# Attention and a two-layer feed-forward on one core: the second layer with the output weights stationary and 256 squares moving

## The chip, the cores and the metric

The kernel runs on one core of a Trainium2 chip, in one launch. The metric is the device time in microseconds (us), the median over several runs. TensorE does the matmuls, VectorE (DVE), ScalarE (ACT) and GpSimd (POOL) the elementwise work; SyncE (SP) issues the DMAs.

## The reference

Four batches of eight heads with 768 positions of 64 numbers attend to a window of their neighbours and to sums over blocks of 32; the 3072 x 512 result then goes through a feed-forward of two layers with a squared ReLU between them. Only the second part is touched by the change:

```python
def _moe_ref(x, w_in, w_out):          # x 3072 x 512, w_in 512 x 2048, w_out 2048 x 512
    h = np.maximum(x @ w_in, 0.0)
    return (h * h @ w_out).astype(np.float32)

x = attn_out.transpose(0, 2, 1, 3).reshape(B * S, H * D)
return _moe_ref(x=x, **moe_kwargs)
```

## The kernel before, in words

**Tiling.** The 3072 tokens are cut into 24 attention tiles g of 128 (six for each batch), and for the feed-forward into 12 groups c of `CT` = 256 tokens (two tiles). The 2048 hidden units are cut into `NF` = 16 blocks f of 128. A unit of work is a pair (c, f): the first layer makes 128 hidden units for 256 tokens, their squares go through the second layer, and the second layer's result of 512 model columns for 256 tokens is summed in PSUM over all 16 blocks f.

**Precision by parts.** x, the weights and the squares are each kept as a high part and a low part of fp32r (`xh`, `xl`; `w_sb[f][:, 0]` and `w_sb[f][:, 1]`; `gh`, `gl`), and each product is the sum of three matmuls: high by high, high by low, low by high. `w_sb[f]` holds w_in in its first 512 columns and w_out of the same f behind them, in `DM:`.

**First layer** (`ffn1`, L348). For each of four blocks of the model dimension and each of the three products: 128 x 128 weights stationary, 256 tokens of `xh` or `xl` moving, into `ph` (hidden unit by token). 12 matmuls of 256 columns a unit.

**Squares** (`relu`, `high_square`, `square`, `low_square`): `r` = max(ph, 0), `gh` = r squared, ph = ph times r, `gl` = ph - gh, split between ScalarE and VectorE. They come out as hidden unit by token, 128 x 256.

**Second layer** (`ffn2`, L389). For each of two tiles of 128 tokens (`tt`) and each of the three products: 128 columns of `gh` or `gl` stationary, the 512 columns of w_out moving, into `o_ps[c][tt]`, a whole PSUM bank of token by model column. 6 matmuls of 512 columns a unit. After the last f, `evict` copies each of the two tiles to SBUF (`ob`) and stores it to 128 rows of the output.

**Order.** The first part of the program follows a list written out by hand (`START`), in which F1, RE, SQ, MU, GL, F2 and EV are a unit's first layer, its squares, its second layer and its eviction. It covers the first two groups and six attention tiles; there an accumulation is parked in SBUF halfway (`parked`) while weights still arrive. After it, `slot(c, f, ...)` runs for the other ten groups, eight times each: the first layer of two units (24 matmuls), then the second layer of the two units of the slot before (`finish`, 12 matmuls), so that the squares of two units are made while TensorE works on others. Steps of later attention tiles (`steps`: scores, softmax, turning, outputs) are hung into the slots. Nothing reorders the program; each engine runs its instructions as they are written.

Of the kernel before, what the change touches and what calls it, by code (L numbers as in the profile page):

```python
# [11 lines left out]
F32 = mybir.dt.float32  # L12
# [8 lines left out]
B, H, S, D = 4, 8, 768, 64  # L21
BLOCK, WINDOW = 32, 16
NB = S // BLOCK
DM, DF = 512, 2048
P = 128
NT = S // P
NPAIR = H // 2
TPC = 2
CT = TPC * P
# [41 lines left out]
def attn_ffn_kernel(ctx: ExitStack, tc: tile.TileContext, q, k, kt, v, vt, v0, w, masks, ident, mean, out):  # L71
    nc = tc.nc
# [8 lines left out]
    ps_o = ctx.enter_context(tc.tile_pool(name="ps_o", bufs=2, space=bass.MemoryType.PSUM))  # L81
# [3 lines left out]
    w_sb = {}  # L85
# [19 lines left out]
    def copy(eng, out, in_):  # L105
        nc.scalar.copy(out=out, in_=in_) if eng is nc.scalar else eng.tensor_copy(out=out, in_=in_)  # L106


    def load_q(g):
        nc.sync.dma_start(out=q_sb[g % 2], in_=q[g // NT, g % NT])  # L110

    def load_k(g):
        nc.sync.dma_start(out=k_sb[g % 2][:, 0:4], in_=k[g // NT, g % NT])

    def load_qk(g):
        load_q(g)
        load_k(g)

    def load_v(g):
        nc.sync.dma_start(out=v_sb[g % 2][0:96], in_=v[g // NT, g % NT])  # L120
# [49 lines left out]
    def place_k(g):  # L170
        nc.vector.tensor_copy(out=k_sb[g % 2][:, 4], in_=ksum.unsqueeze(1).to_broadcast([P, 2, NPAIR, NB]))
# [106 lines left out]
    def softmax(g, h0, h1):  # L278

        for h in range(h0, h1):  # L280
            mask_max(g, h)
            exponentials(h)
# [58 lines left out]
    o_ps, parked = {}, {}  # L341

    def ffn1(c, f):
        ph = ps_h.tile([P, 4, P], F32, name="ph").rearrange("p a b -> p (a b)")[:, 0:CT]
        n = 0
        for cc in range(NC4):
            for w, x in ((0, xh), (1, xh), (0, xl)):
                nc.tensor.matmul(  # L348
                    ph, lhsT=w_sb[f][:, w, cc * P : (cc + 1) * P], rhs=x[c][:, cc, :], start=(n == 0), stop=(n == 3 * NC4 - 1)
                )  # L350
                n += 1
        return ph
# [23 lines left out]
    def squares(ph):  # L376
        r = relu(ph, nc.scalar)
        gh = high_square(r)
        square(ph, r)
        return gh, low_square(ph, gh)  # L380

    def ffn2(c, f, gh, gl, first, last):
        if first:
            o_ps[c] = [ps_o.tile([P, DM], F32, name="o_ps") for _ in range(TPC)]
        for tt in range(TPC):
            ts_ = slice(tt * P, (tt + 1) * P)
            n = 0
            for g_, w in ((gh, 0), (gh, 1), (gl, 0)):
                nc.tensor.matmul(  # L389
                    o_ps[c][tt], lhsT=g_[:, ts_], rhs=w_sb[f][:, w, DM:],  # L390
                    start=(first and n == 0), stop=(last and n == 2),
                )
                n += 1

    def evict(c, f, tt, eng):

        if (c, tt) in parked:
            ob = parked[c, tt]
            nc.vector.tensor_add(out=ob, in0=o_ps[c][tt], in1=ob)
        else:  # L400
            ob = work.tile([P, DM], F32, name="ob", tag="ob", bufs=4)
            copy(eng, ob, o_ps[c][tt])
        if f < NF - 1:
            parked[c, tt] = ob
        else:
            r0 = c * CT + tt * P
            nc.sync.dma_start(out=out[r0 : r0 + P, :], in_=ob)

# [4 lines left out]
    def finish():  # L415

        for p in behind:
            ffn2(*p)
        done = [p[:2] for p in behind if p[-1]]
        behind.clear()  # L420
        return done[0] if done else None

    def slot(c, f, side, last):


        ph = [ffn1(c, f + i) for i in range(2)]
        done = finish()
        for i in range(2):
            for do in side[i]:
                do()  # L430
            behind.append((c, f + i, *squares(ph[i]), f + i == 0, f + i == NF - 1))
        for tt in range(TPC if done else 0):
            evict(*done, tt, nc.scalar)
        for do in last:
            do()
# [35 lines left out]
    def load(what, i):  # L471
        if what == "kv":
            load_kv0(i)
        elif what == "kw":
            load_kv(1, i)
        elif what == "q":
            load_q(i)
        elif what == "k":
            load_k(i)
        elif what == "v":  # L480
            load_v(i)
        elif what == "w":
            load_w(i)
        elif what == "vn":
            vn[i] = room(F32, "vn")[:, 0 : 3 * DM].rearrange("p (t c) -> p t c", c=DM)
            nc.sync.dma_start(out=vn[i], in_=v0[:, 3 * i : 3 * i + 3])
        elif what == "mask":
            nc.sync.dma_start(out=mask_sb, in_=masks.rearrange("m q c -> q m c"))
        elif what == "id":
            nc.sync.dma_start(out=id_sb, in_=ident)  # L490
        else:
            nc.sync.dma_start(out=mean_sb, in_=mean)

    def begin(op, i, j, eng):


        if op == "KS":
            sum_k(0, i)
        elif op == "PK":
            place_k(i)  # L500
        elif op == "SV":
            v_mean[0] = sum_v0([vn[0], vn[1]])
        elif op == "VC":
            place_v0(v_mean[0], i, eng)
        elif op == "KT":
            sum_k(1, i)
        elif op == "VT":
            sum_v(1, i)

        elif op == "S":  # L510
            (scores_kt if i < FROM_KT else scores)(i, 2 * j, 2 * j + 2)
        elif op == "TT":
            mask_max(i, j)
        elif op == "E":
            exponentials(j)
        elif op == "NR":
            inverse(j)
        elif op == "N":
            norm(j, eng)
        elif op == "T":  # L520
            tp[i, j] = turn_pe(i, j)
        elif op == "TC":
            copy(eng, pT[i % 2][:, j * 4 : j * 4 + 4], tp.pop((i, j)))
        elif op == "O":
            outputs(i)
        elif op == "XH":
            high_x(i)
        elif op == "XL":
            low_x(i)

        elif op in ("HI", "LO", "SH", "AD", "CA", "SU"):
            {"HI": sign_w, "LO": round_w, "SH": shift_w, "AD": add_w, "CA": high_w, "SU": low_w}[op](i, eng)

        elif op == "F1":
            ph_of[i] = ffn1(*units[i][:2])
        elif op == "RE":
            r_of[i] = relu(ph_of[i], eng)
        elif op == "SQ":
            g_of[i] = [high_square(r_of[i])]
        elif op == "MU":  # L540
            square(ph_of[i], r_of[i])
        elif op == "GL":
            g_of[i].append(low_square(ph_of.pop(i), g_of[i][0]))
        elif op == "F2":
            c, f, f0, f1 = units[i]
            ffn2(c, f, *g_of.pop(i), f == f0, f == f1 - 1)
        elif op == "EV":
            evict(*units[[4, 15, 26, 31][i]][:2], j, eng)
        else:
            raise AssertionError(op)  # L550

    with tc.manual_schedule(engines=None):
        for token in START.split():
            what, i, j, eng = re.fullmatch(r"(L:[a-z]+|F[12]|[A-Z]+)\.?(\d*)\.?(\d*)([avp]?)", token).groups()
            i, j = int(i or 0), int(j or 0)
            if what.startswith("L:"):
                load(what[2:], i)
            else:
                begin(what, i, j, engines.get(eng))
        tiles = {g: steps(g) for g in range(6, n_g)}  # L560

        def at(side, last, g, step):

            for i in range(2):
                if g in tiles and 0 <= step + i < 12:
                    side[i] += tiles[g][0][step + i]
                    last += tiles[g][1][step + i]

        place_k(7)
        load_q(7)  # L570
        load_k(7)
        load_v(6)
        load_v(7)
        load_qk(8)
        softmax(6, 0, 6)
        behind += [(*units[i][:2], *g_of[i], False, i == 31) for i in (30, 31)]
        for c in range(2, n_c):
            for f in range(0, NF, 2):
                side, last = [[], []], []
                at(side, last, 2 * c + 2, f + (4 if c == 2 else 6))  # L580
                at(side, last, 2 * c + 3, f - 2)
                at(side, last, 2 * c + 4, f - 10)
                slot(c, f, side, last)
        done = finish()
        for tt in range(TPC):
            evict(*done, tt, nc.scalar)


# [65 lines left out]
```

## Time and profile before

| | us |
|---|---|
| three runs | 625.07, 625.56, 627.52 |
| their median | 625.56 |
| the profiled execution's own time, first to last instruction (span) | 624.0 |
| TensorE busy with matmuls in the span | 599.8 |
| TensorE busy with weight loads, beside the matmuls | 537.5 |
| VectorE, ScalarE, GpSimd busy | 411.9, 293.8, 97.4 |
| mean granted TensorE clock | 0.992 |

The three runs are executions without the profiler; the profile is one further execution, for which the span is the time that is known. Matmuls overlap one another, so a line's busy time is the time in which at least one of its matmuls was in flight, and the mean of one is the whole passage of one through the engine. How far apart two matmuls of a row are is read from the start times in the timeline. L348 is the first layer's matmul, L389 the second's.

### The profile page before, as it was taken

What the parts mean: (1) busy time and instruction counts of PE and PEld (TensorE: products, weight loads), DVE (VectorE), ACT (ScalarE), POOL (GpSimd) and SP (SyncE); (2) the same over time, 40 slices, a digit from 0 to 9 for tenths busy, and PEclk for the clock granted to TensorE, in tenths of its full rate; (3) what the DMA queues carried; (4) which work ended last, traced back from release to release, by engine and by line L of the source; (5) the groups of instructions that cost most, each with busy time, mean ns of one, the idle gap of its engine ahead of it and who ended that gap; (6) DMA issues with size and microseconds to landing.
All of it is one profiled execution on the core that took longest, in us unless ns stands there. A gap on an engine that the chain in (4) does not pass through costs nothing.

```text
span 624.0 us, 13374 instructions
## 1 busy us (share of the span) xinstructions
PE 599.8 (96%) x5216; PEld 537.5 (86%) x5216; DVE 411.9 (66%) x1237; ACT 293.8 (47%) x850; POOL 97.4 (16%) x83
## 2 busy tenths in 40 slices
PE   2699999999999999999999999999999999999997
PEld 2588888988989988998988989899889989889996
DVE  4889989768766857757658668567566566563222
ACT  2778887333544353443534444434525525433322
POOL 2555762001210100101201101101101001000000
PEclk9979999999999999999999999999999999999999
DMA  8999610462132231220230321311201301000000
GB/s 286 378 359 326 213 60 21 154 202 99 27 120 70 83 119 50 104 69 35 68 118 37 119 84 70 119 52 48 74 26 44 103 1 26 35 1 2 35 0 35
DMA packets 19855, 60.38 MB, mean 97 GB/s; under 512 B 2768, under 2 KB 2896, under 8 KB 17744
## 3 DMA queue, kind: packets, MB, share of 16 engines
q1 hardware_dynamic: 19792, 59.53, 28.4%
q8 instruction: 41, 0.67, 0.5%
q14 instruction: 22, 0.18, 0.1%
HBM read 53.23 MB, written 6.29 MB: 95 GB/s over the span
## 4 chain that ended last, share of the span: by engine, by line
PE 92%; DMA 3%; DVE 2%; ACT 2%; SPq 0%; issue 0%; DVEq 0%; ACTq 0%
PE ph L348 42%; PE o_ps L389 41%; PE x_ps L317 4%; PE s_ps L241 3%; DMA q_sb<-in_q 2%; DMA mask_sb<-in_masks 1%; PE s_ps L256 1%; PE ph L297 1%; ACT e_sb L276 0%; DVE w_sb L227 0%; DVE e_sb L268 0%; ACT w_sb L106 0%; SPq L152 0%; DVE sm L285 0%; DVE w_raw L216 0%
## 5 line engine op out<-in xcount | busy, mean ns | idle before, releaser
L348 PE MATMUL ph<-xh,w_sb 128*128 128x256 f32 x1536 | 272.6, 280 | 0.2 <-DVE gl L373 0.2
L348 PEld LDWEIGHTS ph<-xh,w_sb 128*128 128x128 f32 x1536 | 238.6, 189 | 9.7 <-issue 3.0
L389 PE MATMUL o_ps<-w_sb,gh 128*128 128x512 f32 x768 | 237.9, 391 | 0.0
L348 PE MATMUL ph<-xl,w_sb 128*128 128x256 f32 x768 | 213.5, 278 | 0.2 <-DVE xl L334 0.2
L389 PEld LDWEIGHTS o_ps<-w_sb,gh 128*128 128x128 f32 x768 | 137.1, 188 | 24.8 <-issue 0.2
L389 PE MATMUL o_ps<-w_sb,gl 128*128 128x512 f32 x384 | 151.4, 394 | 0.9 <-DVE gl L373 0.9
L369 DVE TENSOR_TENSOR ph<-ph,r 128x256 f32<-128x256 f32 x192 | 82.6, 431 | 101.0 <-ACT r L357 98.8
L357 ACT ACTIVATE r<-ph 128x256 f32<-128x256 f32 x180 | 68.0, 378 | 168.1 <-PE ph L348 167.9
L348 PEld LDWEIGHTS ph<-xl,w_sb 128*128 128x128 f32 x768 | 145.1, 189 | 0.4 <-DVE xl L334 0.4
L291 POOL TENSOR_TENSOR e_sb<-e_sb,sm 128x480 f32<-128x480 f32 x43 | 43.5, 1013 | 403.5 <-DVE nmx L268 356.6
L276 ACT ACTIVATE e_sb<-e_sb,nmx 128x120 f32<-128x120 f32 x192 | 73.8, 386 | 67.3 <-DVE nmx L268 67.3
L304 DVE STREAM_TRANSPOSE pT<-e_sb 32x256 f32<-32x256 f32 x216 | 94.2, 436 | 5.1 <-POOL e_sb L291 1.8
L373 DVE TENSOR_TENSOR gl<-ph,gh 128x256 fp32r<-128x256 f32 x192 | 81.5, 425 | 23.3 <-DVE ph L369 0.5
L364 ACT ACTIVATE gh<-r 128x256 fp32r<-128x256 f32 x192 | 80.2, 418 | 12.1 <-DVE r L359 6.1
L389 PEld LDWEIGHTS o_ps<-w_sb,gl 128*128 128x128 f32 x384 | 72.2, 188 | 15.7 <-DVE gl L373 1.3
L334 DVE TENSOR_TENSOR xl<-x_ps,xh 128x512 fp32r<-128x512 f32 x24 | 16.6, 690 | 48.1 <-ACT xh L331 48.1
L268 DVE CUSTOM_DVE_ANT_0 e_sb<-s_ps,mask_sb 128x120 f32<-128x120 f32 x192 | 43.9, 274 | 5.5 <-PE ph L297 1.6
L331 ACT CAST xh<-x_ps 128x512 fp32r<-128x512 f32 x24 | 14.0, 584 | 53.6 <-PE x_ps L317 53.2
L220 POOL TENSOR_TENSOR w_raw<-w_raw 128x1024 int32<-128x1024 int32 x16 | 35.3, 2214 | 24.1 <-ACT w_raw L212 8.7
L317 PEld LDWEIGHTS x_ps<-pT,v_sb 128*64 128x64 f32 x768 | 25.4, 141 | 13.3 <-issue 11.3
L276 ACT ACTIVATION_READ_ACCUMULATOR e_sb<-e_sb,nmx 128x1 f32 x192 | 35.8, 187 | 0.0
L317 PE MATMUL x_ps<-pT,v_sb 128*64 128x64 f32 x768 | 29.0, 229 | 5.3 <-issue 4.0
(47 smaller groups left out, 291.2 us busy)
## 6 DMA issues: line engine op xcount, KB each, us to landing
w_raw<-in_w SPq DMA_DIRECT2D x16, 1024.0 KB, 13.9
v_sb<-in_v SPq DMA_DIRECT2D x24, 384.0 KB, 3.8
k_sb<-in_k SPq DMA_DIRECT2D x20, 384.0 KB, 5.1
kv<-in_kt SPq DMA_DIRECT2D x16, 384.0 KB, 4.8
q_sb<-in_q SPq DMA_DIRECT2D x24, 256.0 KB, 4.1
out<-ob SPq DMA_DIRECT2D x24, 256.0 KB, 2.1
kv<-in_vt SPq DMA_DIRECT2D x12, 384.0 KB, 5.3
vn<-in_v SPq DMA_DIRECT2D x2, 768.0 KB, 10.7
```

The source lines that it names most:

```text
L220: nc.gpsimd.tensor_tensor(out=hi, in0=hi, in1=lo, op=ALU.add)
L268: nc.vector.tensor_tensor_reduce(out=e_sb[:, h, 0:NK], in0=s_ps[g][:, h % 2, h // 2, 0:NK], in1=m, scale=-scale, scalar=3.0e38, op0=ALU.ad ...
L276: nc.scalar.activation(e, e, AF.Exp, bias=nmx[half][:, i : i + 1], scale=-1.0, accum_out=sm[half][:, i : i + 1])
L291: eng.tensor_mul(out=e, in0=e, in1=sm[half].unsqueeze(2).to_broadcast([P, 4, NK]))
L304: nc.vector.transpose(out=pT[g % 2][j * 32 : j * 32 + 32, :, i * 32 : i * 32 + 32], in_=e_sb[i * 32 : i * 32 + 32, :, j * 32 : j * 32 + 32],)
L317: nc.tensor.matmul(xp[o : o + 64, h // 2, s * 64 : s * 64 + 64], lhsT=v_sb[g % 2][:, s, h * 64 : h * 64 + 64], rhs=pT[g % 2][:, h, s * 64 ...
L348: nc.tensor.matmul(ph, lhsT=w_sb[f][:, w, cc * P : (cc + 1) * P], rhs=x[c][:, cc, :], start=(n == 0), stop=(n == 3 * NC4 - 1))
L357: nc.scalar.activation(r, ph, AF.Relu)
L364: nc.scalar.activation(gh, r, AF.Square)
L369: nc.vector.tensor_mul(out=ph, in0=ph, in1=r)
L373: nc.vector.tensor_sub(out=gl, in0=ph, in1=gh.bitcast(F32))
L389: nc.tensor.matmul(o_ps[c][tt], lhsT=g_[:, ts_], rhs=w_sb[f][:, w, DM:], start=(first and n == 0), stop=(last and n == 2),)
```

## The change

The second layer is turned around. Instead of squares stationary and w_out moving, each 128 x 128 block of w_out is stationary, and all 256 tokens of `gh` or `gl` move past it. The result is [model column, token]. Two banks hold it as before, now each with two blocks of 128 model columns side by side, 256 tokens each; the bank `i` is run through all three products before the next, and within a product the two halves `j` take turns. A unit has 12 matmuls of 256 columns instead of 6 of 512. The `start` flag is given with the first half alone. The output in memory has the shape [group, bank, 128, 512], stored in the same 24 pieces of 128 rows by 2 KB, and is transposed on the host after the launch.

```diff
     def ffn2(c, f, gh, gl, first, last):
         if first:
-            o_ps[c] = [ps_o.tile([P, DM], F32, name="o_ps") for _ in range(TPC)]
-        for tt in range(TPC):
-            ts_ = slice(tt * P, (tt + 1) * P)
-            n = 0
-            for g_, w in ((gh, 0), (gh, 1), (gl, 0)):
-                nc.tensor.matmul(
-                    o_ps[c][tt], lhsT=g_[:, ts_], rhs=w_sb[f][:, w, DM:],
-                    start=(first and n == 0), stop=(last and n == 2),
-                )
-                n += 1
+            o_ps[c] = [ps_o.tile([P, DM], F32, name="o_ps") for _ in range(2)]
+        for i in range(2):
+            for n, (g_, w) in enumerate(((gh, 0), (gh, 1), (gl, 0))):
+                for j in range(2):
+                    m = DM + (2 * i + j) * P
+                    nc.tensor.matmul(
+                        o_ps[c][i][:, j * CT : (j + 1) * CT], lhsT=w_sb[f][:, w, m : m + P], rhs=g_,
+                        start=(first and n == 0 and j == 0), stop=(last and n == 2), skip_group_check=True,
+                    )
...
-            r0 = c * CT + tt * P
-            nc.sync.dma_start(out=out[r0 : r0 + P, :], in_=ob)
+            nc.sync.dma_start(out=out[c, tt], in_=ob)
...
-    o = nc.dram_tensor("out_0", (B * S, DM), F32, kind="ExternalOutput").ap()
+    o = nc.dram_tensor("out_0", (B * S // CT, 2, P, DM), F32, kind="ExternalOutput").ap()
...
-    return r.results[0]["out_0"]
+    o = np.asarray(r.results[0]["out_0"]).reshape(B * S // CT, 2, P, 2, CT)
+    return np.ascontiguousarray(o.transpose(0, 4, 1, 3, 2)).reshape(B * S, DM)
```

The order of the work on TensorE, at the first second-layer unit of the start list; the rows name line, operation, output, operands, shape of the moving operand and how many in a row. Rows with a minus are those before, with a plus those now (L393 is the new line of the second layer's matmul):

```order
 L348 MATMUL ph<-xl,w_sb 128x256
-L389 MATMUL o_ps<-w_sb,gh 128x512 x2
-L389 MATMUL o_ps<-w_sb,gl 128x512
-L389 MATMUL o_ps<-w_sb,gh 128x512 x2
-L389 MATMUL o_ps<-w_sb,gl 128x512
+L393 MATMUL o_ps<-gh,w_sb 128x256 x4
+L393 MATMUL o_ps<-gl,w_sb 128x256 x2
+L393 MATMUL o_ps<-gh,w_sb 128x256 x4
+L393 MATMUL o_ps<-gl,w_sb 128x256 x2
 L297 MATMUL ph<-id_sb,e_sb 128x128 x4
```

Each matmul has become two of half the width, in the same place; what stands before and behind is the same. On TensorE at the second unit of a plain slot of the main loop, before, with the engines that a matmul waits for:

```order
L389 MATMUL o_ps<-w_sb,gh 128x512 [waits Activation_49]
L389 MATMUL o_ps<-w_sb,gh 128x512
L389 MATMUL o_ps<-w_sb,gl 128x512 [waits DVE_49]
L389 MATMUL o_ps<-w_sb,gh 128x512 x2
L389 MATMUL o_ps<-w_sb,gl 128x512
L348 MATMUL ph<-xh,w_sb 128x256 x2
```

And the same unit now:

```order
L393 MATMUL o_ps<-gh,w_sb 128x256 [waits Activation_49]
L393 MATMUL o_ps<-gh,w_sb 128x256 x3
L393 MATMUL o_ps<-gl,w_sb 128x256 [waits DVE_49]
L393 MATMUL o_ps<-gl,w_sb 128x256
L393 MATMUL o_ps<-gh,w_sb 128x256 x4
L393 MATMUL o_ps<-gl,w_sb 128x256 x2
L348 MATMUL ph<-xh,w_sb 128x256 x2
```

The waits stand on the first matmul that reads gh and the first that reads gl, as before; behind the unit the next slot's first layer follows. VectorE, ScalarE, GpSimd and SyncE have the same instructions in the same order.

More of the change, by code (lines that the diff above doesn't have):

```diff
@@ L431, in slot @@
             behind.append((c, f + i, *squares(ph[i]), f + i == 0, f + i == NF - 1))
-        for tt in range(TPC if done else 0):
+        for tt in range(2 if done else 0):
             evict(*done, tt, nc.scalar)
@@ L584, in attn_ffn_kernel @@
         done = finish()
-        for tt in range(TPC):
+        for tt in range(2):
             evict(*done, tt, nc.scalar)
```

## The prediction, made before the changed kernel had run

> **What bounds the kernel now.** I read the page's busy shares first, then the table of stretches, then the chain that ended last, and last the timeline of TensorE at a few places. Page and stretches (columns: stretch, then for each engine its busy time in us and its instruction count in brackets, granted clock, share of DMA busy, GB/s):
>
> ```profile
> span 624.0 us, 13374 instructions
> PE 599.8 (96%) x5216; PEld 537.5 (86%) x5216; DVE 411.9 (66%) x1237; ACT 293.8 (47%) x850; POOL 97.4 (16%) x83
> ...
> 60.00:80.00 20.00, 20.00 (x149) 18.10 (x148) 18.08 (x42) 17.81 (x39) 13.59 (x8) 1.00 0.66 227
> ...
> 200.00:300.00 100.00, 100.00 (x865) 89.99 (x858) 68.19 (x220) 44.37 (x144) 8.51 (x9) 1.00 0.26 85
> ...
> 300.00:400.00 100.00, 100.00 (x850) 89.64 (x849) 66.76 (x216) 44.36 (x144) 9.07 (x10) 1.00 0.26 88
> ```
>
> From some 60 us on, TensorE (PE) has matmuls in flight all the time at full clock, DVE has a third of its time free, ACT more than half, DMA three quarters. The end is set by how fast TensorE gets through its queue. Of the chain that ended last, the two layers of the feed-forward part take 83%:
>
> ```profile
> PE ph L348 42%; PE o_ps L389 41%; PE x_ps L317 4%; PE s_ps L241 3%; DMA q_sb<-in_q 2%; DMA mask_sb<-in_masks 1%; PE s_ps L256 1%; PE ph L297 1%; ACT e_sb L276 0%; DVE w_sb L227 0%; DVE e_sb L268 0%; ACT w_sb L106 0%; SPq L152 0%; DVE sm L285 0%; DVE w_raw L216 0%
> ```
>
> L348 is the first layer, L389 the second, which the change rewrites. So the question is one of price: 12 matmuls of 512 columns per two units now, 24 of 256 afterwards. The columns streamed are the same, 6144. The groups give the counts (mean ns of one is its whole passage; matmuls overlap, so it isn't their spacing):
>
> ```profile
> L348 PE MATMUL ph<-xh,w_sb 128*128 128x256 f32 x1536 | 272.6, 280 | 0.2 <-DVE gl L373 0.2
> ...
> L389 PE MATMUL o_ps<-w_sb,gh 128*128 128x512 f32 x768 | 237.9, 391 | 0.0
> L389 PE MATMUL o_ps<-w_sb,gl 128*128 128x512 f32 x384 | 151.4, 394 | 0.9 <-DVE gl L373 0.9
> ...
> L348 PEld LDWEIGHTS ph<-xh,w_sb 128*128 128x128 f32 x1536 | 238.6, 189 | 9.7 <-issue 3.0
> L389 PEld LDWEIGHTS o_ps<-w_sb,gh 128*128 128x128 f32 x768 | 137.1, 188 | 24.8 <-issue 0.2
> ```
>
> The first layer already has the shape that the second is turned into: 128x128 stationary from w_sb, 256 columns of fp32r moving. The kernel carries the price of the new form in itself.
>
> **The price of 256 columns against 512.** Two neighbouring pieces of the chain near 60 us stream the same 15360 columns, once as 60 matmuls of 256, once as 30 of 512:
>
> ```profile
> 58.81 6.83 PE ph L348 x60
> 65.64 6.87 PE o_ps L389 x30
> ```
>
> The 256 form is not dearer: 6.83/60 = 113.8 ns against 6.87/30 = 229.0 ns, half of which is 114.5. The timeline late in the run, where little else happens, shows more (start us, length of the merged rows, engine, line; rows of the first layer come as two xh matmuls and one xl):
>
> ```profile
> 606.37 0.40 PE L348 MATMUL ph<-xh,w_sb 128*128 128x256 f32 x2
> ...
> 606.96 0.28 PE L348 MATMUL ph<-xl,w_sb 128*128 128x256 f32 x1
> 607.08 0.39 PE L348 MATMUL ph<-xh,w_sb 128*128 128x256 f32 x2
> ...
> 608.78 0.39 PE L348 MATMUL ph<-xh,w_sb 128*128 128x256 f32 x2
> ...
> 609.12 0.62 PE L389 MATMUL o_ps<-w_sb,gh 128*128 128x512 f32 x2
> ...
> 611.86 0.40 PE L348 MATMUL ph<-xh,w_sb 128*128 128x256 f32 x2
> ```
>
> From 607.08 (7th matmul) to 608.78 (22nd) lie 15 matmuls: 1.70/15 = 113.3 ns each. From 606.37 to 606.96 lie the first five after a run of 512s: 0.59/5 = 118 ns each, 24 ns in all above the steady pace. The 12 of 512 take 611.86 - 609.12 = 2.74 us, 228 to 229 ns each. So a pair of steady 256s (226.7 ns) beats one 512 (229.0) by 2.3 ns, and on top of it a first layer that follows a second one starts with five slow matmuls. That start isn't caused by other engines:
>
> ```profile
> 608.37 0.43 DVE L369 TENSOR_TENSOR ph<-ph,r 128x256 f32<-128x256 f32 x1 [3.14 <-ACT r L357]
> ...
> 607.96 0.38 ACT L357 ACTIVATE r<-ph 128x256 f32<-128x256 f32 x1 [3.30 <-PE ph L348]
> ```
>
> DVE had been idle for 3.14 us before 608.37 and ACT for 3.30 us before 607.96, so both stood still while the five slow ones ran. What is different there is what TensorE did just before: 512s, or weights taken from gh and gl. Between the units f and f+1 inside a first-layer run (256 to 256, another PSUM bank, another w_sb tile) the pace stays 113.3; the 15 matmuls measured above cross that point.
>
> A rule that speaks against the change: the Trainium skill, "Perfetto Trace Analysis", section "Matmuls", holds that larger matmuls are more efficient than smaller ones, and "TensorE: Matmul & The Clock Gate", section "Back-to-back issue gap", gives the isolated spacing as N/2.4 + 2.5 ns, a fixed part paid once per matmul. By it the 1152 added matmuls would cost 1152 x 2.5 = 2.9 us (an estimate from that page). The trace has the opposite sign: its fixed part, twice 113.3 less 229.0, is -2.3 ns.
>
> **The change part by part.**
> - Second-layer matmuls: 768 + 384 = 1152 of 512 become 2304 of 256. At the steady paces 1152 x 0.2290 = 263.8 us becomes 2304 x 0.1133 = 261.0 us: **-2.8 us**. No row shows w_sb stationary against gh moving, so bounds: below, the 113.3; above, every one as slow as the five after a 512, 118 ns, 271.9 us, +8.1. I take 113.3, since the first layer in long runs is nearest in every respect (weights from the same tiles, same shape and type), and the x60 piece shows no slowing with length.
> - The slow start of a first layer behind a second one: the main loop has 80 slots of 24 + 12; in 19 score or output matmuls stand between, and the start table has about 10 more such borders, 71 in all by the timeline. At 24 to 26 ns each, 71 x 0.025 = **-1.8 us** if the cause is the 512s, 0 if it lies in the switch of layers. I take it as gone, because 256 to 256 borders inside the first layer are free.
> - Weight loads: 1152 more. Each takes 188 ns by its row but they are spaced 113 ns in the first layer and hidden there under the matmul before; the same cover stands in the second layer, so 0. Without that cover this would be the 118 ns case.
> - Waits: gh and gl were stationary and are now moving; the same first matmul of a unit waits for them, and gl is wanted after as many columns (1024 = 2 x 512 = 4 x 256). The wait list has one such stall in the whole run, 0.9 us for gl (row above), early. 0.
> - The evictions (128x512 copies and adds from the same two o_ps tiles, the first whole after half of a unit, as before) and the 24 stores of 256 KB in rows of 2 KB are unchanged; both hidden but for the last pair, which keeps its length. 0. SP, POOL, DVE and ACT keep their order.
> - Instruction supply: 2304 more TensorE instructions:
>
> ```profile
> q8 instruction: 41, 0.67, 0.5%
> ```
>
> 41 packets of 16 KB in 624 us; a fifth more is nothing, and the x60 piece, which asks for instructions at the new pace, isn't starved. 0.
>
> What is late next: nothing. A slot of two units goes from 5.49 to 5.44 us, and DVE with 68.19 of 100 us has room. Sum: 624.0 - 2.8 - 1.8 = 619.4 us of span. The runs before were 625.07, 625.56 and 627.52; their median lies 1.6 above the span of the profile, and I keep that distance: 619.4 + 1.6 = **621.0 us**, 0.7% faster.
>
> **The rivals.**
> - *Only the pace changes.* The slow start belongs to the switch of layers (other PSUM tile, other moving tile), not to the 512s: -2.8 alone, 622.8 us, within 0.5%. For: no row separates width from the layer switch. Against: changing bank and weight tile inside the first layer costs nothing.
> - *No gain at all.* What makes a 512 take 229 instead of 226.7 is not its width but that its operand or its PSUM bank is what it is (both halves of an o_ps bank written, where the first layer writes one half). Then the 256s go at 114.5: 625.6 us. For: first and second layer differ in that as well as in width. Against: nothing direct.
> - *Slower: a cost per matmul in the new form.* If the loads of w_out slices, with nothing but 256s to hide under, come late by the 5 ns that the first five after a 512 show, 2304 x 118 = 271.9 us, +8.1: 633.7 us. It decides from 115.8 ns on ((263.8 + 3.1)/2304). For: the first layer always had second-layer stretches between, so a stream with 256s only for hundreds of us isn't shown. Against: 60 in a row at 113.8 including their start, with loads hidden throughout. The fixed cost of the Trainium skill ("TensorE: Matmul & The Clock Gate", section "Back-to-back issue gap") would end here too, at 625.6 + 2.9 = 628.5 us, an estimate from that page's figure.
>
> **How the numbers follow.** Some 0.5% (3.1 us) is about what a measurement here can tell from no change. Both terms gone: 0.53, at 621.0. Pace alone: 0.19, at 622.8. No gain: 0.14, at 625.6. Slower, by whatever cost per matmul: 0.14, 628 to 634. Faster by over 0.5% means below 622.4: nearly all of the first case and a third of the second, whose runs scatter round it: 0.56. Same: 0.31. Slower: 0.13. The range takes the first three cases with some scatter of the runs, 619.6 to 626.6; its own range for the first alone is 619.6 to 622.2.
>
> **What would show it.** In the profile after: the second layer's timeline rows 113.3 ns apart (24 in 2.72 us instead of 12 in 2.75); the first five matmuls of a first layer behind a second one at 113 instead of 118; a plain slot of 5.44 us; the stretches still with PE fully busy at clock 1.00; weight loads near 2304 x 2 with unchanged idle of DVE and ACT. Wrong would be: a pace of 114.5 or more in the second layer, slow starts that stay, a granted clock below 1.00 under the denser loads, or a new stall of TensorE on gh or gl.

## The result and the profile after

| | us |
|---|---|
| before, median of 4 (beside the changed kernel) | 625.48 |
| changed, four executions | 634.88, 634.96, 635.27, 636.10 |
| changed, median | 635.12 |
| ratio to before, with its 95% interval | 1.0159 [1.0142, 1.0175] |
| span of the profiled execution, before and after | 624.0, 633.2 |

The change made the kernel 1.6% slower, where 0.7% faster was forecast. Where one program's executions fall into two groups of times below, the ratio is taken over the short ones alone, and the single times are given. The page's head and shares of the changed kernel:

```profile
span 633.2 us, 15671 instructions
PE 609.1 (96%) x6368; PEld 597.5 (94%) x6368; DVE 410.9 (65%) x1237; ACT 295.4 (47%) x850; POOL 97.3 (15%) x83
```

VectorE, ScalarE and GpSimd are as busy as before; TensorE is busy for the same 96% of a longer span. The wait list has no new stall (0.9 us on gl, as before), and the granted clock is 1.00 in the long stretches (stretch, busy time of each engine with its instructions in brackets, clock, DMA share, GB/s):

```profile
140.00:300.00 160.00, 160.00 (x1675) 157.36 (x1674) 110.00 (x344) 68.00 (x217) 15.82 (x18) 1.00 0.23 75
300.00:600.00 300.00, 300.00 (x3028) 296.21 (x3027) 180.85 (x577) 126.44 (x395) 24.66 (x27) 1.00 0.17 55
```

So the time lies in the spacing of the matmuls. The chain near 60 us, at the place that the prediction had taken its price from, has exactly the forecast price, 60 matmuls in 6.80 us, 113.3 ns each, in both layers, and without the five slow ones at the layer's head (start, length, piece):

```profile
57.72 6.80 PE ph L348 x60
64.52 6.80 PE o_ps L393 x60
```

The start list has short slow stretches already (12 matmuls in 1.41 us, three times from 82 to 86 us). At 148 us one begins that lasts:

```profile
139.85 2.72 PE o_ps L393 x24
142.57 2.72 PE ph L348 x24
145.29 2.72 PE o_ps L393 x24
148.01 0.98 PE s_ps L241 x32
148.99 3.02 PE ph L348 x24
152.01 2.83 PE o_ps L393 x24
...
161.77 2.83 PE ph L348 x24
```

24 matmuls take 2.72 us ahead of the break with the score matmuls and 2.83 us behind it (the 3.02 holds the restart itself). From there on both layers, not the second alone, go at the slower pace. In the timeline at 302 us:

```profile
302.37 0.63 PE L393 MATMUL o_ps<-gh,w_sb 128*128 128x256 f32 x4
...
308.02 0.64 PE L393 MATMUL o_ps<-gh,w_sb 128*128 128x256 f32 x4
```

48 matmuls in 5.65 us, 117.7 ns each (117.8 over all the matmuls between the breaks at 200 and 222 us), where 5.44 us had been forecast for the slot. It ends as suddenly as it began, at the last break of the program, the outputs of the last attention tile:

```profile
568.22 2.83 PE o_ps L393 x24
571.05 1.08 PE x_ps L317 x32
572.13 2.94 PE ph L348 x24
575.07 2.72 PE o_ps L393 x24
577.79 2.72 PE ph L348 x24
```

Between the two switches lie 136 half slots of 24 matmuls: 136 x 24 x (117.7 - 113.3) ns = 14.4 us. The forecast span of 619.4 and these 14.4 make 633.8; measured are 633.2. That is the whole difference but for 0.6 us.

### The profile page after: what moved, and what is told of

It is laid out like the page before. It is cut to its first block, busy times and chain, and to the rows that moved or that the text cites. A ratio compares the mean times of both kernels' runs of the same rounds, so it can differ in the third digit from the quotient of the medians.

```text
span 633.2 us, 15671 instructions
## 1 busy us (share of the span) xinstructions
PE 609.1 (96%) x6368; PEld 597.5 (94%) x6368; DVE 410.9 (65%) x1237; ACT 295.4 (47%) x850; POOL 97.3 (15%) x83
## 4 chain that ended last, share of the span: by engine, by line
PE 92%; DVE 3%; DMA 2%; ACT 1%; issue 1%; SPq 1%; POOL 0%; DVEq 0%; POOLq 0%
PE ph L348 42%; PE o_ps L393 41%; PE x_ps L317 4%; PE s_ps L241 3%; DMA w_raw<-in_w 2%; PE ph L297 1%; DVE w_sb L227 0%; PE s_ps L256 0%; DVE v_sb L106 0%; DVE sm L285 0%; ACT w_sb L106 0%; DVE e_sb L268 0%; SPq L152 0%; DVE xl L334 0%; DVE pT L106 0%
## 5 line engine op out<-in xcount | busy, mean ns | idle before, releaser
L348 PE MATMUL ph<-xh,w_sb 128*128 128x256 f32 x1536 | 277.2, 282 | 0.3 <-DVE gl L373 0.3
L393 PE MATMUL o_ps<-gh,w_sb 128*128 128x256 f32 x1536 | 242.2, 280 | 0.0
L348 PEld LDWEIGHTS ph<-xh,w_sb 128*128 128x128 f32 x1536 | 234.6, 189 | 3.8 <-issue 3.0
L393 PEld LDWEIGHTS o_ps<-gh,w_sb 128*128 128x128 f32 x1536 | 206.4, 189 | 0.2 <-issue 0.2
L393 PE MATMUL o_ps<-gl,w_sb 128*128 128x256 f32 x768 | 152.2, 280 | 0.9 <-DVE gl L373 0.9
L348 PEld LDWEIGHTS ph<-xl,w_sb 128*128 128x128 f32 x768 | 147.0, 191 | 0.4 <-DVE xl L334 0.4
L393 PEld LDWEIGHTS o_ps<-gl,w_sb 128*128 128x128 f32 x768 | 117.7, 189 | 1.1 <-DVE gl L373 1.1
```

The source lines that it names most:

```text
L348: nc.tensor.matmul(ph, lhsT=w_sb[f][:, w, cc * P : (cc + 1) * P], rhs=x[c][:, cc, :], start=(n == 0), stop=(n == 3 * NC4 - 1))
L393: nc.tensor.matmul(o_ps[c][i][:, j * CT : (j + 1) * CT], lhsT=w_sb[f][:, w, m : m + P], rhs=g_, start=(first and n == 0 and j == 0), stop= ...
```

## The experiments

The theory that these rows suggest: a stream of nothing but 256s has two paces that hold themselves, 113.3 and 117.8 ns, and which one it has is settled where the stream is joined on to matmuls of another shape. The rivals: the turned operand roles, the two halves of a bank in turn, load, other engines.

A half slot is one layer's 24 matmuls in a slot. A break is a place where score or output matmuls stand in the stream of 256s. A joint is any place where the stream starts behind a break or behind an added matmul, or where one layer follows the other.

### Width without the turn

```diff
...
-    o_ps[c][tt], lhsT=g_[:, ts_], rhs=w_sb[f][:, w, DM:],
+    for j in range(2): o_ps[c][tt][:, j*CT:(j+1)*CT], lhsT=g_[:, ts_], rhs=w_sb[f][:, w, DM+j*CT : DM+(j+1)*CT]
```

> The old roles (squares stationary, w_out moving), but each matmul of 512 columns cut into two of 256, the two halves of the bank in turn: the width of the change without its turn. Theory (a pace that holds itself): a stream of nothing but 256s runs at one of two paces, 113.3 or 117.8 ns a matmul, in both layers alike; which one is settled where the stream starts again behind score or output matmuls, and it holds until the next such break. Then this kernel shows the two paces too, both layers always at the same one, and ends between 621 us (all fast) and 637 us (all slow). Rival (roles): w_out as stationary or gh and gl as moving operand is what makes the matmuls late; then here no stretch of 117.8 ns appears, the first layer keeps 113.3, and the time is 620 to 623 us. Rival (halves of a bank in turn): second layer at 117.8 or more from the start, first layer at 113.3.

Measured: 633.81 to 636.14 us, median 634.46, ratio 1.0163 [1.0145, 1.0181]. The chain at 200 us (L390 is the second layer's matmul here):

```profile
200.72 3.02 PE ph L348 x24
203.74 2.82 PE o_ps L390 x24
...
212.22 2.73 PE ph L348 x24
214.95 2.72 PE o_ps L390 x24
217.68 2.83 PE ph L348 x24
```

With the old roles and the new width the loss is the same as that of the whole change. So the turned roles are not needed for the slow pace; the width is enough. The first layer is slow and fast together with the second. One thing went against the theory, by which a pace holds until the next break: here it also changes in mid-stream, where a first layer follows a second one. From 175 us on, four half slots are slow, two fast and two slow between one break and the next.

### The halves of a bank one after the other

```diff
-            for n, (g_, w) in enumerate(((gh, 0), (gh, 1), (gl, 0))):
-                for j in range(2):
+            for j in range(2):
+                for n, (g_, w) in enumerate(((gh, 0), (gh, 1), (gl, 0))):
```

> The changed kernel with the loops over products and halves exchanged: the three products of one half of a bank in a row, then those of the other half, so that consecutive matmuls add into the same half. Theory (a pace that holds itself): nothing in it touches the pace; both paces appear again, 621 to 637 us by where the slow one is caught. Rival (halves of a bank in turn): the slow stretches vanish, 113.3 ns throughout, 619 to 622 us.

Measured: 620.16, 621.35, 637.12 and 637.22 us, ratio of the short ones 0.9939 [0.9921, 0.9958]. The same program ended twice at 620 to 621 and twice at 637, and at nothing between. The profiled execution is a short one (span 619.6): its stream was slow at 140 us, behind the break with the scores alone it was fast, and it stayed so over all later breaks:

```profile
145.83 2.83 PE o_ps L393 x24
148.65 0.98 PE s_ps L241 x32
149.63 2.93 PE ph L348 x24
152.56 2.72 PE o_ps L393 x24
```

Both times are those of the theory. Taking the halves in turn is not needed for the slow pace, since both the slow stretch and the long outcome are there without it.

### The changed kernel once more

No edit.

> The changed kernel once more, unaltered. In the two halves_apart paces one and the same program ended at 620 or 637 us from one execution to the next. Theory (a pace that is settled at a start of the stream and handed on): this one can end near 620 too, but its first four executions all lay at 635; I expect 634 to 636 us in most, and if one of them is caught in the fast pace, 620 to 621 us and nothing between. Rival (a cost of the change itself): always 634 to 636 us.

Measured: 636.25, 635.21, 634.24 and 622.77 us. The changed kernel itself has the short outcome too, one time in the eight executions of it that were timed, the four of the result and these four (at 622.77, some 2 us above the 620 to 621 expected). The 1.6% are not a price of the change in itself.

### No breaks

```diff
-        tiles = {g: steps(g) for g in range(6, n_g)}
+        tiles = {}
-    ... rhs=x[c][:, cc, :]
+    ... rhs=x[min(c, 2)][:, cc, :]
```

> The changed kernel without the attention steps of tiles 6 to 23 in the main loop (scores, softmax, outputs and their loads are left out, and groups 3 to 11 take the x of group 2): from some 140 us on TensorE has nothing but 256s until the end. Theory (a pace that holds itself): whatever pace it has at its last start behind other matmuls (113.3 ns at that place in the changed kernel) it has to the end, so the main loop runs at one pace throughout, most likely 5.44 us a slot, and the whole ends near 575 to 580 us. Rival (load): 256s with a weight load each draw so much that TensorE slows to 117.8 ns after some time at full rate; then the pace drops here too, at 150 us or later, with no break before it. Rival (other engines): softmax work of VectorE and ScalarE or the DMAs disturb the reads; then no stretch is slow.

Measured: 580.54 us, span 578.7, and in the chain, from 140 us to the end, nothing but pieces like these:

```profile
281.36 2.72 PE o_ps L393 x24
284.08 2.72 PE ph L348 x24
```

For over 430 us TensorE did nothing but 256s with a weight load each, at 113.3 ns. Load alone does not bring the slow pace. Softmax work is missing here, so other engines were not excluded by this run; one_512 below shows the slow pace without that work.

### A 512 at the head of every slot

```diff
-    def ffn1(c, f):
+    def ffn1(c, f, wide=False):
...
+        if wide:
+            nc.tensor.matmul(ph, lhsT=w_sb[f][:, 0, 0:P], rhs=w_sb[f][:, 0, DM:], start=True, stop=True)
...
-        ph = [ffn1(c, f + i) for i in range(2)]
+        ph = [ffn1(c, f + i, i == 0) for i in range(2)]
```

> The changed kernel with one more matmul of 512 columns at the head of each slot of the main loop, ahead of the first layer, its result overwritten by the first layer. It adds 80 x 0.229 = 18.3 us. Theory (a pace that holds itself, and 512s knock the stream out of the slow one, as five slow matmuls and then the fast pace behind each run of 512s in the kernel before show): no slot stays at 117.8 ns, each has at most some five slow matmuls; 619.5 + 18.3 + 1.8 = 639.6 us of span, 641 us. Rival (the slow pace comes from something else than the stream's start): slow slots stay, 633.2 + 18.3 = 651.5 us of span, 653 us. A part of the theory: if one 512 isn't enough and a run of them is needed, slow slots stay too, but which ones are slow changes.

Measured: 650.69 us, span 648.9, near the rival's 651.5. The chain shows why:

```profile
199.48 0.98 PE s_ps L241 x32
200.46 0.43 PE ph L346
200.89 2.75 PE ph L351 x24
203.63 2.72 PE o_ps L396 x24
206.35 0.23 PE ph L346
206.58 2.83 PE ph L351 x24
209.41 2.83 PE o_ps L396 x24
212.24 0.23 PE ph L346
212.47 2.83 PE ph L351 x24
```

(L346 is the added matmul, L351 and L396 the two layers.) Right behind a break the 512 leads to the fast pace; in mid-stream it leads to the slow one, and from slow to slow. So the part of the theory that a 512 knocks the stream out of the slow pace fell. What stayed: the pace is settled at a joint, within the first few matmuls behind it, and holds until the next. In this run each kind of joint gave the same pace each time: the 20 added matmuls behind a break led to the fast one, the 60 in mid-stream to the slow one.

### One 512 in an unbroken stream

On top of the edits of no_attention:

```diff
+        if (c, f) == (6, 0):
+            nc.tensor.matmul(ph, lhsT=w_sb[f][:, 0, 0:P], rhs=w_sb[f][:, 0, DM:], start=True, stop=True)
```

> As no_attention (attention of tiles 6 to 23 left out, groups 3 to 11 take the x of group 2), with a single matmul of 512 columns, its result overwritten, put once into the unbroken stream, at the head of group 6. no_attention ran at 113.3 ns from 140 us to the end, and in break_512 a 512 in the middle of a fast stretch was always followed by a slow one. Theory (the timing of a joint settles the pace, and it holds): fast up to group 6, then 117.8 ns for all the 2304 matmuls behind it: one matmul of 0.23 us costs 0.23 + 2304 x 0.0045 = 10.6 us, 589.3 us of span against 578.7. Rival (the slow pace is a state of load or of the engines' neighbours): the 512 costs its 0.23 us, 578.9 us of span.

Measured: 590.86 us, span 589.0 (589.3 by the theory, 578.9 by the rival).

```profile
305.58 2.72 PE ph L351 x24
308.30 2.72 PE o_ps L396 x24
311.02 0.23 PE ph L346
311.25 2.83 PE ph L351 x24
314.07 2.83 PE o_ps L396 x24
```

One matmul of 0.23 us makes the remaining 278 us slow, to the last matmul: 10.3 us more than without it. No attention work, no DMA of attention data and no other engine's step begins there: ScalarE had been idle for 3.53 us up to 312.70, VectorE for 3.37 us up to 313.12. That speaks against load, time and neighbours as the cause, and shows that the pace is kept by the stream itself. This run and no_attention are one execution each; the switch lies inside this one.

### A 512 behind the breaks only

The same added matmul, only in slots that follow a break (`fresh` is filled by the score and output matmuls of the main loop). The trace has 19 of them; behind the start list there is none.

```diff
...
+        if c > 1 and fresh:
+            fresh.clear()
+            nc.tensor.matmul(ph, lhsT=w_sb[f][:, 0, 0:P], rhs=w_sb[f][:, 0, DM:], start=True, stop=True)
```

> The changed kernel with one more matmul of 512 columns, its result overwritten, at the head of the first layer, but only in the slots that follow a break (20 of 80). With one in every slot the stream was fast behind each 512 that stood right behind a break and slow behind those in mid-stream. Theory (the start settles the pace and it holds): every stretch between two breaks is fast but for some five matmuls, 619.6 + 20 x 0.229 + 20 x 0.025 = 624.7 us of span, 626.3 us. Rival (the pace comes from elsewhere): slow stretches stay, 633.2 + 4.6 = 637.8 us of span, 639 us.

Measured: 632.32 to 633.63 us, ratio 1.0117 [1.0101, 1.0134]. Neither number came out. From 175 us on the stretches between breaks alternate, one slow, the next fast (L349 is the added matmul, L354 and L399 are the two layers):

```profile
217.03 2.72 PE ph L354 x24
219.75 2.72 PE o_ps L399 x24
222.47 1.08 PE x_ps L317 x32
223.55 0.98 PE s_ps L241 x32
224.53 0.43 PE ph L349
224.96 2.83 PE ph L354 x24
227.79 2.83 PE o_ps L399 x24
```

The same joint gives fast behind slow and slow behind fast. So the pace ahead of a break matters too: something of it is carried through the 2.1 us of other matmuls. Behind the breaks with outputs alone, at 155 and 568 us, the fast pace stayed.

### A matmul of 64 columns behind the breaks

In place of the 512 of wide_restart, behind the same 19 breaks:

```diff
+            nc.tensor.matmul(ph[:, 0:64], lhsT=w_sb[f][:, 0, 0:P], rhs=w_sb[f][:, 0, DM : DM + 64], start=True, stop=True)
```

> As wide_restart, but the added matmul has 64 columns. Theory (the timing of the start settles the pace): the start is shifted by a few tens of ns, always by the same, so all breaks of the main loop lead to the same pace; if to the fast one, 619.6 + 20 x 0.06 = 620.8 us of span, 622.4 us; if to the slow one, 635 to 638 us; a mixture would speak against it. Rival (only a wide matmul sets the fast pace): slow, 635 to 638 us.

Measured: ten executions, 622.09 to 624.78 us, ratio 0.9973 [0.9957, 0.9988]. In the profiled one the stream was slow up to the first such joint, at 149 us, and every stretch behind one is fast (at 149 us the break alone can do that, as halves_apart shows). Work was added, and the kernel became 11 us shorter than the changed one.

### The break with scores alone taken out

The first attention tile of the main loop runs one slot earlier, so that outputs and scores stand together at every break.

```diff
+        for n in (4, 5):
+            for do in tiles[6][0][n]: do()
...
-                at(side, last, 2 * c + 2, f + (4 if c == 2 else 6))
+                at(side, last, 2 * c + 2, f + 6)
```

> The changed kernel with the first attention tile of the main loop one slot earlier, so that its outputs stand in the same place as the scores of tile 7: there is no break with score matmuls alone any more, all breaks are outputs and then scores. In the changed kernel the stream was at 113.3 ns up to the break with scores alone at 148 us and at 117.8 ns behind it, and each later break with outputs and scores handed the pace on. Theory (the break with scores alone flips the pace): without it the stream stays at 113.3 ns from 140 us to the end, 619 to 622 us. Rival (any break may flip it, by its timing): slow stretches appear at other breaks, 621 to 637 us. Rival (a cost of the change itself): 634 to 636 us.

Measured: nine executions from 625.75 to 630.75 us and one of 639.78; ratio of the former 1.004 [1.0024, 1.0056]. In the profiled one (span 624.9) all half slots from the first break on take 2.72 us, but for those that hold a restart, as the theory says. But the time is not 619 to 622: the earlier tile isn't ready, and from 137 to 149 us the chain leaves TensorE for ScalarE, GpSimd and VectorE. TensorE waits 1.1 us for gl and 3.1 us for the eviction `ob` there, and the 24 matmuls behind the longer wait take 4.58 instead of 2.72 us. These are not at the slow pace: the granted clock was 0.50 from 150.4 to 153.7 us, and the matmuls were 213 to 214 ns apart.

```profile
143.84 0.44 DVE ph L369
144.38 0.42 DVE gl L373
...
149.65 4.58 PE o_ps L393 x24
```

And the one execution of 639.78, which was not profiled, lies about as far above the others as a slow pace to the end would put it. If that is what it was, the break with scores alone isn't the only thing that brings the slow pace.

### Breaks in the middle of a slot, and breaks in the other order

The score and output matmuls moved between the two layers of the next slot:

```diff
         ph = [ffn1(c, f + i) for i in range(2)]
+        for do in held: do()
+        held.clear()
         done = finish()
...
-        for do in last: do()
+        held.extend(last)
```

> The changed kernel with the score and output matmuls moved from the end of a slot to the middle of the next one, between its first layer and its second. No work is added. Theory (the timing of a joint settles the pace): same matmuls, other joints, so the pace may be settled either way, but it holds between breaks, both layers alike: 620 to 622 us or 634 to 637 us, or a repeating pattern of both between. Rival (first layer behind the breaks is what is slow): 113.3 ns throughout, 620 us.

Measured: 620.29, 621.16, 634.72 and 635.37 us. The scores set ahead of the outputs:

```diff
-                slot(c, f, side, last)
+                slot(c, f, side, lasts[0] + lasts[1] + lasts[2])   # youngest tile first
```

> The changed kernel with scores ahead of outputs at each break, instead of behind them. No work is added. Theory (the timing of a joint settles the pace): the stream starts again behind output matmuls instead of score matmuls, at another timing; it holds its pace from break to break: 620 to 622 us if fast, 634 to 637 us if slow, between them if the breaks alternate as in wide_restart. Rival (the pace is handed on by any break, only the one with scores alone flips it): as the changed kernel, 634 to 636 us in most executions.

Measured: 619.90, 636.59, 636.84 and 636.88 us. No work was added or taken away in either, and both have the two outcomes, so moving the breaks doesn't avoid the slow pace.

The traces say more than the times. Five profiled executions have no added matmul and keep the break with scores alone (after, again, halves_apart and the two here), and in all five that break turned the pace over. In after, again and breaks_swapped the stream was fast ahead of it and slow behind it, and the spans were 633 to 635 us; in halves_apart and breaks_midslot it was slow ahead and fast behind, and the spans were 619 to 620. Each later break with outputs and scores handed the pace on, and behind the last break, with outputs alone, all five were fast. That is what the rival of breaks_swapped says, and three of its four times, at 636.6 to 636.9, lie just above the rival's 634 to 636. The pace ahead of that break is settled when the stream starts at 137 us, behind a wait for VectorE (`xl`). So in these five a fast start led to the long outcome. Why that break turns the pace over is not shown, nor is it seen in the executions without a profile.

### The matmul of 64 columns in the first group only

```diff
-        if c > 1 and fresh:
+        if c == 2 and fresh:
```

> As nudge_64, but the matmul of 64 columns stands only behind the three breaks of the main loop's first group (behind the start list, behind the scores alone, behind the outputs alone). In nudge_64 it set the fast pace behind each break at a cost of 0.11 us each. Theory (the pace is handed on by breaks of outputs and scores): fast from 150 us to the end without any further nudge, 17 x 0.11 = 1.9 us less than nudge_64: 620 to 622 us in all executions. Rival (every break decides anew, by its own timing): slow stretches come back behind later breaks, 625 to 637 us.

Measured: six executions, 620.69 to 623.21 us, median 621.49, against 625.53 before on the same chip: ratio 0.9932 [0.9917, 0.9948]. Three added matmuls of 64 columns, behind the breaks at 148, 155 and 173 us, suffice; the later breaks hand the fast pace on. (The expectation counts the end of the start list among the three; the trace has none there.) In its trace the stream was fast ahead of the break with scores alone and stayed fast, where the five traces without the added matmul turn over. This version is 0.7% shorter than the kernel before. Its stretches, beside those of the changed kernel above:

```profile
140.00:300.00 160.00, 160.00 (x1719) 157.40 (x1719) 112.10 (x360) 71.27 (x235) 16.21 (x18) 1.00 0.25 82
300.00:600.00 300.00, 300.00 (x3109) 296.27 (x3108) 182.75 (x573) 126.38 (x393) 24.68 (x27) 1.00 0.16 52
```

TensorE is busy for the same 160.00 and 300.00 us, at the same clock, with the same share of weight loads; only the counts differ, 3109 against 3028 matmuls in 300 us.

## Why the prediction was wrong

- *What bounds the kernel*: right. TensorE's pace sets the end before and after.
- *The price of 256 against 512*: here it failed. The step took 113.3 ns as the price of a 256 and kept 118 ns as a far bound, on the ground that 60 in a row showed no slowing with length. Length is indeed not it: no_attention held 113.3 ns for over 430 us. But 118 ns is a second pace of the same stream, in which it stayed for 420 us. The sum also has no term for a slower first layer: its 2304 matmuls stay at their old pace without a reason, and half of the 136 slow half slots are first layers. In the trace of before the second pace stood in plain sight: behind each run of 512s the first layer began with five matmuls of it.
- *The slow start of a first layer*: the term was read as a start-up cost that the 512s cause, and so as a gain when they go. With the fast pace it is gone, as forecast: 2.72 us for 24, and nudge_first ends at a span of 619.9, halves_apart at 619.6, against the forecast 619.4. So the sum is right for a stream that stays fast. What the reading missed is that the five ended: behind a run of 512s the stream left the slow pace by itself each time, and in the changed kernel no joint did so from 148 to 571 us. That the runs of 512s are what kept the slow pace short is likely but not shown; a single 512 in mid-stream brought the slow pace instead (break_512, one_512).
- *Waits, evictions, instruction supply at nothing*: right. There is no new stall, and TensorE has matmuls in flight throughout.
- *Weight loads at nothing*: right at the fast pace. At the slow one the trace has a mark that the prediction had no reason to look for: in one_512 every third weight load took 192 ns behind the added matmul (736 of 2208 from 320 to 580 us) and none did ahead of it, where all took 187 or 188 ns. Whether that is a cause or a consequence is open.
- *The rival "slower"*: its time was near (+8.1 from 118 ns; +9.2 measured in the span), but by luck. It had the second layer alone slow for the whole run; measured was both layers slow for most of it, 14.4 us above the forecast. Its mechanism, loads that come late because there is nothing but 256s to hide under, fails as a standing cost: with nothing but 256s the stream held 113.3 ns in no_attention. Its ground for doubt, that a stream of 256s alone wasn't shown for hundreds of us, was the right one and should have widened the range; its chance of 0.14 was too small.
- *The rule of the Trainium skill*, "Perfetto Trace Analysis", section "Matmuls", that larger matmuls are more efficient, has the sign of the first result, but no fixed price for each matmul shows: nudge_first, with twice the second-layer matmuls, is shorter than before. The same page of the Trainium skill, section "Identifying the Most-Contended Engine", advises two measures for TensorE, the share of the peak arithmetic rate that is reached and the share of weight loads; the second reads 157.36 of 160 us in the slow stretch and 157.40 in the fast one and tells nothing of the difference.

What has these two paces, and what at a joint selects one, stays open. The runs show that the pace is settled at joints, kept by the stream, and differs between executions of one program.

## What to carry to other kernels

A matmul's price is a spacing of starts, and it should be read over the whole run, in each layer and behind each kind of joint; two spacings of one shape in one trace, however short one of them is, mean two possible prices, and the range has to hold the kernel's time at either. Before a 1% result of a kernel bound by TensorE is laid to an edit, count matmuls in stretches that are fully busy, and time several executions: one program can end at two times. Where it does, a small matmul at the joint can be worth far more than it costs: here three of 64 columns were followed by the short outcome in six executions of six, against one of eight without them.

## What the runs showed of the hardware

Streams of 128x128 fp32r weights with 256 columns moving ran at 113.3 or 117.8 ns a matmul at a granted clock of 1.00, for over 430 us at the one (no_attention) and 420 us at the other (the changed kernel). A single 512 in the stream turned the one into the other for the remaining 278 us (one_512). With 64 columns behind the first breaks the fast pace followed, whether the stream ahead was slow (nudge_64) or fast (nudge_first). At the slow pace every third weight load took 192 ns, at the fast one all took 187 or 188 (one_512). In the kernel before, 512s ran at 229 ns, more than two fast and less than two slow 256s.
